# Decode block on one core: output weights of group six behind the last values, second MLP weights in 8, 3, 2, 1 chunks, group two's last query rows by eight DMA engines

## The chip, the cores and the metric

The kernel runs on one core of a Trainium2 chip. The metric is the device time of one execution in microseconds (us), lower is better; the time before is the median of three runs. Loads go through 16 DMA engines of the core; the compute engines are PE (matrix), DVE (vector), ACT (scalar) and POOL. SP does no arithmetic here: it issues the large loads and the final store.

## The reference

One decode step of a transformer block in float32, for 4 tokens (batch B = 4, one query each) and a model width D of 448: grouped attention with 16 query heads over 8 key/value groups of width 256, on the last 1024 entries of the cache, then an MLP of width F = 1792. Each part has a layer norm ahead of it and a residual sum behind it.

```python
def _A_ref(x, k_cache, v_cache, wq, wo):
    W = min(4096, max(256, Sk // 4))          # 1024
    q = (x @ wq) -> heads
    k = k_cache[:, :, Sk - W:, :];  v = v_cache[:, :, Sk - W:, :]
    p = softmax(q @ k^T * Dh ** -0.5)
    return (p @ v) -> rows @ wo
def _B_ref(x, w1, b1, w2, b2):
    return gelu(_layernorm(x) @ w1 + b1) @ w2 + b2
h = x + _A_ref(_layernorm(x), k_cache, v_cache, wq, wo)
out = h + _B_ref(_layernorm(h), w1, b1, w2, b2)
```

Nearly all of the bytes are the keys and values: 8 groups, each 4 MB of keys and 4 MB of values, read once.

## The kernel before

**Loads.** `load` fills a tile of 128 partitions from a packed array in HBM, on SP's queue, in one DMA or in several pieces (L52). There are two rings of two tiles each: kind "k" and kind "v". A load into a tile waits until the work on the tile's earlier contents is done, and each DMA on the queue also waits for the semaphore of the one eight places before it. For group g, `load_k` brings the keys and, in the same rows, the query weights of the next groups (1792 columns); `load_v` brings the values and, in the same rows, the group's output weights `wo` (1792 columns behind the 8192 of the values). The rows of these arrays in HBM are 9984 floats long (39936 bytes).

The query weights of one group are a 448 x 512 matrix. Its first 384 rows lie as 3 x 512 columns on 128 partitions; the last 64 rows are folded onto 128 partitions and 256 columns. Group one is the exception: its last 64 rows come as 64 partitions of 512 columns, by two small DMAs (L73) whose source is shaped (8, 4, 512) with a gap behind each four, so that the outermost dimension is 8. The four small loads of the residual rows and biases (`rows`, L132) go by ACT's queue at the start.

**The loop over the groups.** `scores` (L182) multiplies queries and keys, `transpose_p` turns the softmax, `project_q` (L159) makes the queries of the group two ahead, `values` (L219) multiplies with the values in four pairs of chunks, `transposed_output` (L236 to L244) scales and transposes the result, and `add_output` (L248) adds its product with the output weights into the accumulator `acc`. The last two groups, six and seven, are written out behind the loop.

**The order behind the loop.** The order on PE is the order of the program text; the loads are issued in text order on SP's queue: keys of seven, values of six with their `wo`, values of seven in three pieces, `wo` of seven, the first MLP weights `w1` in two pieces, the second `w2` in three pieces of 8, 4 and 2 chunks (D columns each). PE runs: values of six; the first pair of seven's values; transposition and output of six (L248); a copy of `acc` to `accs` on ACT (L321); two more pairs of seven's values; `add_quadrants` (L256), which folds `accs` into the four-quadrant layout of `last`; the last pair; the transposition of seven; the output of seven added to `last` (L335). Then come the layer norm (L358 to L374), the first MLP product `pu` (L388), the gelu (L402), transposes, and the second product. Its chunks 0 to 7 go into `pa` (L421), which ACT copies to `pas` (L425); chunks 8 to 13 go directly into `py` (L431), and after chunk 9 `add_quadrants` folds `pas` into `py` (L256). The residual is added at L437 and the result stored at L438. `keep_warm` (L308) puts matmuls without a use into waits so that PE's clock stays up.

Of the kernel before, what the change touches and what calls it, by code (L numbers as in the profile page):

```python
# [8 lines left out]
F32 = mybir.dt.float32  # L9
# [6 lines left out]
B, D = 4, 448  # L16
HQ, HKV, SK, DH = 16, 8, 4096, 256
REP = HQ // HKV
W = min(4096, max(256, SK // 4))
F = 1792  # L20
P = 128
H = P // 2
ND = 4
NKC = W // P
NFC = F // P
FQ = F // 4
Q = 32
CACHE = NKC * B * DH
WEIGHTS = 4 * D
# [1 line left out]
SCALE = DH ** -0.5  # L31

@with_exitstack
def block_kernel(ctx: ExitStack, tc, rows, wq0, k0, wq1, kq, vo, w1, w2, out):
    nc = tc.nc
    const = ctx.enter_context(tc.tile_pool(name="const", bufs=1))
    ring = ctx.enter_context(tc.tile_pool(name="ring", bufs=2))
# [10 lines left out]
    def load(kind, src, pieces, name):  # L48
        t = ring.tile([P, CACHE + WEIGHTS], F32, tag=kind, name=name)
        at = 0  # L50
        for n in pieces:
            nc.sync.dma_start(t[:, at : at + n], src[:, at : at + n])  # L52
            at += n
        return t


    def wq_parts(t, last=None):
        parts = [(a, yT[:, a, :], slice(0, 512), t[:, a * 512 : (a + 1) * 512]) for a in range(3)]
        if last is not None:
            return parts + [(3, yT[:H, 3, :], slice(0, 512), last)]  # L60
        for i in range(2):
            parts.append((3, yT[:, 3 + i, :], slice(i * 2 * P, (i + 1) * 2 * P), t[:, 3 * 512 :]))
        return parts


    def load_k(g):
        half = CACHE // 2
        if g == 0:
            t = load("k", k0, (CACHE + 3 * 512,), "k0")


            for i in range(2):
                nc.sync.dma_start(  # L73
                    wq1_last[i * Q : (i + 1) * Q, :], wq1[i].rearrange("e (p c) -> e p c", c=512)[:, :4, :]
                )
            last = wq1_last
        else:
            pieces = (CACHE + WEIGHTS,) if g + 1 < HKV else (CACHE,)
            t = load("k", kq[g - 1], pieces, f"k{g}")
            last = None  # L80
        kt = [t[:, i * half : (i + 1) * half].rearrange("p (c b k) -> p c b k", c=2, b=B) for i in range(2)]
        return kt, wq_parts(t[:, CACHE:], last) if g + 1 < HKV else None


    def load_v(g):
        pieces = (CACHE + WEIGHTS,)
        if g == HKV - 1:
            pieces = (CACHE // 4, CACHE // 2, CACHE // 4, WEIGHTS)
        t = load("v", vo[g], pieces, f"v{g}")
        v = t[:, :CACHE].rearrange("p (c b d) -> p c b d", c=NKC, b=B)  # L90
        return [v[:, c : c + 2] for c in range(0, NKC, 2)], t[:, CACHE:].rearrange("p (j e) -> p j e", j=4)


    ident = const.tile([P, P], F32, name="ident")
# [11 lines left out]

    yT = const.tile([P, ND + 1, Q], F32, name="yT")
    nc.vector.memset(yT, 0.0)
    wq1_last = const.tile([H, 512], F32, name="wq1_last")
    zT = const.tile([P, ND, Q], F32, name="zT")  # L110
    nc.vector.memset(zT, 0.0)

# [62 lines left out]
    def scores(g, kt):  # L175
        mx = work.tile([P, 2], F32, tag="mx", name=f"mx{g}")
        halves = []
        for h in range(2):
            s = ps_s.tile([P, 512], F32, tag="s", name=f"s{g}_{h}")
            for c in range(2):  # L180
                for b in range(B):
                    nc.tensor.matmul(  # L182
                        s[b * Q : (b + 1) * Q, :], qT[g % 2][:, c, b, :], kt[h][:, c, b, :],
                        start=(c == 0), stop=(c == 1),
                    )
            nc.vector.reduce_max(mx[:, h : h + 1], s, axis=AX.X)  # L186
            halves.append(s)
        nm = work.tile([P, 1], F32, tag="nm", name=f"nm{g}")
        nc.vector.tensor_max(nm, mx[:, 0:1], mx[:, 1:2])
        nc.vector.tensor_scalar_mul(nm, nm, -SCALE)  # L190
        p = work.tile([P, 2 * 512], F32, tag="p", name=f"p{g}")
        sums = work.tile([P, 2], F32, tag="sums", name=f"sums{g}")
        for h in range(2):
            nc.scalar.activation(  # L194
                p[:, h * 512 : (h + 1) * 512], halves[h], AF.Exp, bias=nm, scale=SCALE,
                accum_out=sums[:, h : h + 1],
            )
        rec = work.tile([P, 1], F32, tag="rec", name=f"rec{g}")
        nc.vector.tensor_add(rec, sums[:, 0:1], sums[:, 1:2])
        nc.vector.reciprocal(rec, rec)  # L200
        return p, rec
# [14 lines left out]
    def values(g, vt, po, pairs=range(NKC // 2)):  # L216
        for c in pairs:
            for b in range(B):
                nc.tensor.matmul(  # L219
                    po[b * Q : (b + 1) * Q], pT[g % 2][:, c, b, :], vt[c][:, :, b, :],  # L220
                    start=(c == 0), stop=(c == NKC // 2 - 1),
                )
# [5 lines left out]
    def columns(t, j):  # L228
        if j < 3:
            return t[:, j * P : (j + 1) * P].rearrange("p (i c) -> p i c", i=2)  # L230
        return t[:, None, 3 * P :].to_broadcast([t.shape[0], 2, H])


    def transposed_output(g, po, rec):
        o = work.tile([P, 2, DH], F32, tag="o", name=f"o{g}")
        nc.vector.tensor_scalar_mul(o, po, rec)  # L236
        pt = ps_m.tile([P, 2, 2, P], F32, tag="m", name=f"pot{g}")
        for i in range(2):
            for c in range(2):
                nc.tensor.transpose(pt[:, i, c], o[:, i, c * P : (c + 1) * P], ident)  # L240
        dst = oT[g % 2].rearrange("p (r c) q -> p c r q", r=REP)[:, :, :, :B]
        src = pt.rearrange("p i c (b q) -> p i c q b", b=B)
        nc.vector.tensor_copy(dst, src[:, 0, :, :REP])  # L243
        nc.vector.tensor_add(dst, dst, src[:, 1, :, REP : 2 * REP])  # L244

    def add_output(g, wt):
        for i in range(4):
            nc.tensor.matmul(  # L248
                acc[i * Q : (i + 1) * Q, :], oT[g % 2][:, i, :], wt[:, i, :],
                start=(g == 0), stop=(g == HKV - 2),  # L250
            )


    def add_quadrants(dst, t, start):
        for j in range(4):
            nc.tensor.matmul(dst[j * Q : (j + 1) * Q], sel, columns(t, j), start=start, stop=False)  # L256

    def po_tile(g, pool=ps_o, tag="o"):
        return pool.tile([P, 2, DH], F32, tag=tag, name=f"po{g}")


    t = load("v", wq0, (WEIGHTS + ND * B,), "wq0")
    wqt = wq_parts(t[:, :WEIGHTS])
    xT = t[:, WEIGHTS : WEIGHTS + ND * B].rearrange("p (a b) -> p a b", a=ND)
    d = work.tile([P, ND, B], F32, tag="d", name="d_x")
# [11 lines left out]
    p, rec = scores(0, kt)  # L277
    project_q(1, wqt)
    transpose_p(0, p)
    for g in range(HKV - 2):  # L280
        kt, wqt = load_k(g + 1)
        vt, wot = load_v(g)
        p, rec_next = scores(g + 1, kt)
# [8 lines left out]

    g = HKV - 2
    kt, _ = load_k(g + 1)
    vt, wot = load_v(g)
    vt_last, wo_last = load_v(g + 1)
    t = load("k", w1, (2 * F, F + F // 2), "w1")
    w1t = [t[:, a * F : min((a + 1) * F, 3 * F + F // 2)] for a in range(ND)]
    t = load("k", w2, (8 * D, 4 * D, 2 * D), "w2")
    w2t = [t[:, c * D : (c + 1) * D] for c in range(NFC)]  # L300
    p, rec_last = scores(g + 1, kt)

# [3 lines left out]
    def keep_warm(n, warm):  # L306
        for _ in range(n):
            nc.tensor.matmul(warm[:Q], idle[:, :Q], idle, start=True, stop=True)  # L308
# [6 lines left out]
    po_last = po_tile(g + 1, ps_t, "t")  # L315
    warm = ps_t.tile([P, 512], F32, tag="t", name="warm")
    values(g + 1, vt_last, po_last, range(0, 1))
    transposed_output(g, po, rec)
    add_output(g, wot)
    accs = once.tile([P, D], F32, tag="u", name="accs")  # L320
    nc.scalar.copy(accs, acc)  # L321

    keep_warm(2, warm)
    values(g + 1, vt_last, po_last, range(1, 3))
    last = ps_s.tile([P, 512], F32, tag="s", name="last")[:, :P]
    ph = last.rearrange("p (i c) -> p i c", i=2)
    add_quadrants(ph, accs, True)
    values(g + 1, vt_last, po_last, range(3, 4))

    keep_warm(2, warm)  # L330
    transposed_output(g + 1, po_last, rec_last)
    keep_warm(1, warm)
    for i in range(4):
        for j in range(4):
# [27 lines left out]
    d = once.tile([P, P], F32, tag="dh", name="dh")  # L362
# [21 lines left out]
    for a in range(ND):  # L384
        m = Q if a == 0 else B
        for j in range(4):
            rows, w = w1_part(a, j)
# [29 lines left out]
    first = 8  # L417
    pa = ps_w.tile([P, D], F32, tag="acc", name="pa")
    for c in range(first):
        j, m = c % 4, Q if c < 4 else B  # L420
# [6 lines left out]
    for c in range(first, NFC):  # L427
        for j in range(4):
            m, n = (Q, 2) if c == first else (B, 2 if j < 3 else 1)
            w = columns(w2t[c], j) if n == 2 else w2t[c][:, None, 3 * P :]  # L430
            nc.tensor.matmul(  # L431
                py[j * Q : j * Q + m, :n, :], gT[:, c, :m], w, start=(c == first), stop=(c == NFC - 1),
            )
        if c == first + 1:
            add_quadrants(py, pas, False)
    res = once.tile([P, P], F32, tag="res", name="res")
    nc.vector.tensor_add(res, py.rearrange("p i c -> p (i c)"), hb)  # L437
# [67 lines left out]
```

## Time and profile before

| | us |
|---|---|
| median of 3 runs | 214.57 |
| the runs, lowest to highest | 214.44 to 214.58 |
| the profiled execution, first to last instruction | 212.9 |
| PE busy in it | 137.9 |
| DVE busy | 39.2 |
| ACT busy | 21.0 |
| bytes read from HBM | 88.26 MB, 415 GB/s over the span |

The profile is of one execution. Its span leaves out what lies around the first and last instruction, 1.7 us. A line of its timeline gives the start and length of a group of instructions in us, the engine, the line of the kernel, the operation with output and inputs, and in brackets how long the engine had been idle and what ended that. PEld is PE's loading of stationary operands, which runs beside its matmuls; each float32 matmul of the program appears as two in the trace. In a row of stretches stand the stretch, the busy time and count of each engine, the granted PE clock, the mean busy share of the DMA engines and GB/s. A packet is counted in the stretch in which it starts, so the share can pass 1. In the list of DMA queues, q1 holds SP's loads, q8 and q14 the fetches of instructions; the columns are packets, MB and share of the sixteen engines' time.

### The profile page before, as it was taken

How to read it: one execution, taken by the hardware profiler on the slowest of the kernel's cores; microseconds unless marked ns; L12 is line 12 of the kernel's file. 1: busy time of each engine (PE TensorE's matmuls, PEld its weight loads, DVE VectorE, ACT ScalarE, POOL GpSimd, SP SyncE). 2: the span in 40 equal slices, each digit the busy share in tenths (PEclk: the TensorE clock that was granted, in tenths of full speed). 3: DMA queues.
4: the chain of work that ended last, by engine and by line, in shares of the span. 5: the costliest groups of instructions: out<-in, count | busy, mean ns of one | idle time of the engine just before them, and what ended most of it. 6: DMA issues, size and time to landing. Idle time of an engine off the chain costs nothing.

```text
span 212.9 us, 2306 instructions
## 1 busy us (share of the span) xinstructions
PE 137.9 (65%) x971; PEld 49.1 (23%) x971; DVE 39.2 (18%) x167; ACT 21.0 (10%) x52; POOL 5.6 (3%) x17
## 2 busy tenths in 40 slices
PE   0456868093886739583986348382948476798994
PEld 0322233021231212211231113120222123234432
DVE  1420324001130202210130104110230231022320
ACT  0210213000030000300030003000030001000311
POOL 6100000000000000000000000000000000000110
PEclk9999999669597966969599859979797999699999
DMA  7999998999989999999999999999989999999991
GB/s 291 426 399 469 398 465 378 459 465 390 458 378 465 465 390 458 398 446 465 390 458 405 443 465 386 465 413 428 461 375 468 440 428 390 417 418 433 424 390 60
DMA packets 3865, 88.46 MB, mean 415 GB/s; under 512 B 448, under 2 KB 576, under 8 KB 1168
## 3 DMA queue, kind: packets, MB, share of 16 engines
q1 hardware_dynamic: 3824, 88.29, 96.9%
q8 instruction: 7, 0.11, 0.2%
q10 hardware_dynamic: 32, 0.05, 0.1%
q14 instruction: 2, 0.02, 0.0%
HBM read 88.26 MB, written 0.07 MB: 415 GB/s over the span
## 4 chain that ended last, share of the span: by engine, by line
DMA 85%; PE 11%; DVE 2%; issue 0%; SPq 0%
DMA v<-vo 65%; DMA w<-w 12%; DMA k<-k 8%; PE po L219 8%; PE acc L248 1%; DVE o L236 1%; PE pot L240 1%; PE py L431 1%; DVE oT L243 0%; DVE oT L244 0%; SPq L52 0%; DVE res L437 0%; PE py L256 0%
## 5 line engine op out<-in xcount | busy, mean ns | idle before, releaser
L182 PE MATMUL s<-k,qT 128*32 128x512 f32 x256 | 42.3, 822 | 24.7 <-DMA k<-kq 22.6
L219 PE MATMUL po<-v,pT 128*32 128x512 f32 x256 | 40.0, 772 | 19.6 <-DMA v<-vo 19.6
L186 DVE TENSOR_REDUCE mx<-s 128x1 f32<-128x512 f32 x16 | 11.1, 691 | 67.4 <-PE s L182 67.4
L182 PEld LDWEIGHTS s<-k,qT 128*32 128x32 f32 x256 | 10.0, 146 | 54.7 <-issue 29.4
L219 PEld LDWEIGHTS po<-v,pT 128*32 128x32 f32 x256 | 10.7, 135 | 42.3 <-issue 31.4
L161 ACT COPY qs<-pq 128x512 f32<-128x512 f32 x8 | 4.7, 586 | 135.8 <-PE pq L159 135.8
L236 DVE TENSOR_SCALAR o<-po,rec 128x512 f32<-128x512 f32 x8 | 6.0, 750 | 60.2 <-PE po L219 60.2
L194 ACT ACTIVATE p<-s,nm 128x512 f32<-128x512 f32 x16 | 10.9, 690 | 18.4 <-DVE nm L190 18.4
L207 PE MATMUL ppt<-ident,p 128*128 128x128 f32 x64 | 10.5, 286 | 2.0 <-ACT p L194 1.7
L165 PE MATMUL pqt<-ident,qs 128*128 128x128 f32 x32 | 5.7, 304 | 6.2 <-ACT qs L161 6.2
L240 PE MATMUL pot<-ident,o 128*128 128x128 f32 x32 | 5.2, 286 | 5.7 <-DVE o L236 5.7
L248 PE MATMUL acc<-v,oT 128*32 128x448 f32 x56 | 6.7, 551 | 3.3 <-DVE oT L244 3.3
L207 PEld LDWEIGHTS ppt<-ident,p 128*128 128x128 f32 x64 | 6.7, 140 | 6.0 <-ACT p L194 6.0
L159 PE MATMUL pq<-k,yT 128*32 128x512 f32 (+1 forms) x66 | 7.3, 515 | 0.0
L308 PE MATMUL warm<-idle 128*32 128x512 bf16 x25 | 7.3, 382 | 0.0
L240 PEld LDWEIGHTS pot<-ident,o 128*128 128x128 f32 x32 | 3.3, 140 | 13.0 <-DVE o L236 13.0
L165 PEld LDWEIGHTS pqt<-ident,qs 128*128 128x128 f32 x32 | 3.6, 150 | 10.9 <-ACT qs L161 9.1
L153 POOL TENSOR_TENSOR r<-ve_r,mhalf 128x1 f32<-128x1 f32 x2 | 1.1, 544 | 191.9 <-DVE ve_r L152 191.9
L211 DVE COPY pT<-ppt 128x16 f32<-128x16 f32 x32 | 4.7, 170 | 4.7 <-PE ppt L207 4.7
L159 PEld LDWEIGHTS pq<-k,yT 128*32 128x32 f32 x66 | 3.1, 110 | 6.1 <-issue 4.8
L138 PE MATMUL pm_x<-wq,mean 128*128 128x12 f32 x2 | 0.6, 363 | 5.8 <-DMA wq<-wq 5.8
L167 DVE TENSOR_REDUCE sm<-pqt 128x16 f32<-128x64 f32 x8 | 1.8, 225 | 13.0 <-PE pqt L165 13.0
(101 smaller groups left out, 60.9 us busy)
## 6 DMA issues: line engine op xcount, KB each, us to landing
v<-vo SPq DMA_DIRECT2D x7, 4992.0 KB, 31.8
k<-kq SPq DMA_DIRECT2D x6, 4992.0 KB, 32.0
k<-k SPq DMA_DIRECT2D x1, 4864.0 KB, 16.3
k<-kq SPq DMA_DIRECT2D x1, 4096.0 KB
w<-w SPq DMA_DIRECT2D x2, 1792.0 KB
v<-vo SPq DMA_DIRECT2D x2, 1024.0 KB, 22.2
v<-vo SPq DMA_DIRECT2D x1, 2048.0 KB
w<-w SPq DMA_DIRECT2D x1, 1344.0 KB
```

The lines of the kernel that those rows point to most:

```text
L159: nc.tensor.matmul(pq[j * Q : (j + 1) * Q, cols], y, w, start=True, stop=True)
L161: nc.scalar.copy(qs, pq)
L165: nc.tensor.transpose(pt[:, i, :], qs[:, i * P : (i + 1) * P], ident)
L182: nc.tensor.matmul(s[b * Q : (b + 1) * Q, :], qT[g % 2][:, c, b, :], kt[h][:, c, b, :], start=(c == 0), stop=(c == 1),)
L186: nc.vector.reduce_max(mx[:, h : h + 1], s, axis=AX.X)
L194: nc.scalar.activation(p[:, h * 512 : (h + 1) * 512], halves[h], AF.Exp, bias=nm, scale=SCALE, accum_out=sums[:, h : h + 1],)
L207: nc.tensor.transpose(pt[:, c, :], p[:, (4 * h + c) * P : (4 * h + c + 1) * P], ident)
L219: nc.tensor.matmul(po[b * Q : (b + 1) * Q], pT[g % 2][:, c, b, :], vt[c][:, :, b, :], start=(c == 0), stop=(c == NKC // 2 - 1),)
L236: nc.vector.tensor_scalar_mul(o, po, rec)
L240: nc.tensor.transpose(pt[:, i, c], o[:, i, c * P : (c + 1) * P], ident)
L248: nc.tensor.matmul(acc[i * Q : (i + 1) * Q, :], oT[g % 2][:, i, :], wt[:, i, :], start=(g == 0), stop=(g == HKV - 2),)
L308: nc.tensor.matmul(warm[:Q], idle[:, :Q], idle, start=True, stop=True)
```

## The change

Three parts, with the host packing that goes with each.

- The values of groups six and seven lie in an array `v` of their own, with rows of 8192 floats (32768 bytes). The output weights of six and of seven are packed ahead of `w1` in an array `ow`, and are loaded in this order behind seven's last values: `wo` of six, `wo` of seven, `w1` in two pieces. On PE all of seven's values come before the output of six, and the fold of `accs` comes behind seven's transposition.
- `w2` is loaded in pieces of 8, 3, 2 and 1 chunks, and `pas` is folded into `py` after chunk 10.
- The last 64 rows of group two's query weights come, as group one's did, in two small DMAs of the (8, 4, 512) shape, behind the keys of group one; the rows of those keys lose 256 columns.

```diff
+    def load_last(n):
+        t = wq_last[:, n, :]
+        for i in range(2):
+            nc.sync.dma_start(
+                t[i * Q : (i + 1) * Q, :], wql[n, i].rearrange("e (p c) -> e p c", c=512)[:, :4, :]
+            )
+        return t
...
     def load_k(g):
...
-            for i in range(2):
-                nc.sync.dma_start(
-                    wq1_last[i * Q : (i + 1) * Q, :], wq1[i].rearrange("e (p c) -> e p c", c=512)[:, :4, :]
-                )
-            last = wq1_last
+            last = load_last(0)
+        elif g == 1:
+            t = load("k", kq[0], (CACHE + 3 * 512,), "k1")
+            last = load_last(1)
...
     def load_v(g):
-        pieces = (CACHE + WEIGHTS,)
-        if g == HKV - 1:
-            pieces = (CACHE // 4, CACHE // 2, CACHE // 4, WEIGHTS)
-        t = load("v", vo[g], pieces, f"v{g}")
...
+        if g < HKV - 2:
+            t = load("v", vo[g], (CACHE + WEIGHTS,), f"v{g}")
+        else:
+            pieces = (CACHE,) if g == HKV - 2 else (CACHE // 4, CACHE // 2, CACHE // 4)
+            t = load("v", v[g - HKV + 2], pieces, f"v{g}")
...
-    vt, wot = load_v(g)
-    vt_last, wo_last = load_v(g + 1)
-    t = load("k", w1, (2 * F, F + F // 2), "w1")
+    vt, _ = load_v(g)
+    vt_last, _ = load_v(g + 1)
+    t = load("k", ow, (WEIGHTS, WEIGHTS, 2 * F, F + F // 2), "ow")
+    wot, wo_last = (wo_parts(t[:, i * WEIGHTS : (i + 1) * WEIGHTS]) for i in range(2))
+    t = t[:, 2 * WEIGHTS :]
     w1t = [t[:, a * F : min((a + 1) * F, 3 * F + F // 2)] for a in range(ND)]
-    t = load("k", w2, (8 * D, 4 * D, 2 * D), "w2")
+    t = load("k", w2, (8 * D, 3 * D, 2 * D, D), "w2")
...
     transposed_output(g, po, rec)
+    keep_warm(2, warm)
+    values(g + 1, vt_last, po_last, range(1, 4))
+
+    keep_warm(2, warm)
     add_output(g, wot)
     accs = once.tile([P, D], F32, tag="u", name="accs")
     nc.scalar.copy(accs, acc)
-
-    keep_warm(2, warm)
-    values(g + 1, vt_last, po_last, range(1, 3))
+    transposed_output(g + 1, po_last, rec_last)
     last = ps_s.tile([P, 512], F32, tag="s", name="last")[:, :P]
     ph = last.rearrange("p (i c) -> p i c", i=2)
     add_quadrants(ph, accs, True)
-    values(g + 1, vt_last, po_last, range(3, 4))
-
-    keep_warm(2, warm)
-    transposed_output(g + 1, po_last, rec_last)
     keep_warm(1, warm)
...
-        if c == first + 1:
+        if c == first + 2:
             add_quadrants(py, pas, False)
```

More of the change, by code (lines that the diff above doesn't have):

```diff
@@ L33, in block_kernel @@
 @with_exitstack
-def block_kernel(ctx: ExitStack, tc, rows, wq0, k0, wq1, kq, vo, w1, w2, out):
+def block_kernel(ctx: ExitStack, tc, rows, wq0, k0, wql, kq, vo, v, ow, w2, out):
     nc = tc.nc
@@ L82, in load_k, with wo_parts @@
         return kt, wq_parts(t[:, CACHE:], last) if g + 1 < HKV else None
+    def wo_parts(t):
+        return t.rearrange("p (j e) -> p j e", j=4)
     def load_v(g):
-        pieces = (CACHE + WEIGHTS,)
-        if g == HKV - 1:
-            pieces = (CACHE // 4, CACHE // 2, CACHE // 4, WEIGHTS)
-        t = load("v", vo[g], pieces, f"v{g}")
-        v = t[:, :CACHE].rearrange("p (c b d) -> p c b d", c=NKC, b=B)
-        return [v[:, c : c + 2] for c in range(0, NKC, 2)], t[:, CACHE:].rearrange("p (j e) -> p j e", j=4)
+        if g < HKV - 2:
[3 more added lines that the diff above has]
+            t = load("v", v[g - HKV + 2], pieces, f"v{g}")
+        vt = t[:, :CACHE].rearrange("p (c b d) -> p c b d", c=NKC, b=B)
+        return [vt[:, c : c + 2] for c in range(0, NKC, 2)], wo_parts(t[:, CACHE:])
     ident = const.tile([P, P], F32, name="ident")
@@ L108, in block_kernel @@
     nc.vector.memset(yT, 0.0)
-    wq1_last = const.tile([H, 512], F32, name="wq1_last")
+    wq_last = const.tile([H, 2, 512], F32, name="wq_last")
     zT = const.tile([P, ND, Q], F32, name="zT")
@@ L470 @@
     k0 = np.concatenate([k[0], wq[1][:, : 3 * 512]], axis=1)
-    wq1 = np.asarray(A_wq).reshape(D, HKV, 512)[3 * P :, 1].reshape(2, 8, 4 * 512)
-    wq1 = np.concatenate([wq1, np.zeros((2, 8, 512), np.float32)], axis=2)
-    vo = np.concatenate([v, wo], axis=2)
-    w1 = packed(np.asarray(B_w1))
+    wql = np.asarray(A_wq).reshape(D, HKV, 512)[3 * P :, 1:3].transpose(1, 0, 2).reshape(2, 2, 8, 4 * 512)
+    wql = np.concatenate([wql, np.zeros((2, 2, 8, 512), np.float32)], axis=3)
+    vo = np.concatenate([v[: HKV - 2], wo[: HKV - 2]], axis=2)
+    v = v[HKV - 2 :]
+    ow = np.concatenate([wo[HKV - 2], wo[HKV - 1], packed(np.asarray(B_w1))], axis=1)
     w2 = np.asarray(B_w2).reshape(4, FQ, D)
@@ L489 @@
     arrays = {
-        "rows": rows, "wq0": np.concatenate([wq[0], xT], axis=1), "k0": k0, "wq1": wq1, "kq": kq, "vo": vo, "w1": w1, "w2": w2,
+        "rows": rows, "wq0": np.concatenate([wq[0], xT], axis=1), "k0": k0, "wql": wql, "kq": kq, "vo": vo, "v": v, "ow": ow, "w2": w2,
     }
```

## The prediction, made before the changed kernel ran

> **What bounds the kernel now.** I read the page first, then the chain of waits from its end, then the DMA share in stretches, then the timeline of the last stage.
>
> ```profile
> span 212.9 us, 2306 instructions
> PE 137.9 (65%) x971; PEld 49.1 (23%) x971; DVE 39.2 (18%) x167; ACT 21.0 (10%) x52; POOL 5.6 (3%) x17
> DMA  7999998999989999999999999999989999999991
> q1 hardware_dynamic: 3824, 88.29, 96.9%
> q8 instruction: 7, 0.11, 0.2%
> q14 instruction: 2, 0.02, 0.0%
> DMA 85%; PE 11%; DVE 2%; issue 0%; SPq 0%
> ```
>
> The DMA engines are busy in every slice but the last, and 85% of the chain is DMA. So the time is the loads' bytes over their rate, plus what follows the last landing. PE at 65% has room. The chain's last pieces:
>
> ```profile
> 145.34 36.79 DMA v<-vo
> 182.14 26.22 DMA w<-w
> 208.41 0.64 PE py L431 x13
> 209.05 0.17 PE py L256 x6
> 209.22 0.97 PE py L431 x19
> 210.21 0.29 DVE res L437
> ```
>
> The second MLP weights are the last load, and only 2 us of arithmetic stand behind it. How the engines run out of work (columns at the end: DMA share, GB/s):
>
> ```profile
> 132.00:144.00 12.00, 7.70 (x48) 2.69 (x46) 2.04 (x11) 1.04 (x4) 0.00 (x0) 0.86 1.03 443
> 206.50:207.00 0.50, 0.50 (x8) 0.13 (x4) 0.00 (x0) 0.03 (x1) 0.00 (x0) 1.00 0.92 380
> 207.00:207.50 0.50, 0.50 (x12) 0.13 (x4) 0.00 (x0) 0.00 (x0) 0.00 (x0) 1.00 0.75 308
> 207.50:208.00 0.50, 0.50 (x8) 0.00 (x0) 0.00 (x0) 0.00 (x0) 0.00 (x0) 1.00 0.61 244
> 208.00:208.50 0.50, 0.13 (x7) 0.09 (x8) 0.00 (x0) 0.35 (x1) 0.00 (x0) 1.00 0.60 244
> 208.50:209.00 0.50, 0.50 (x24) 0.50 (x28) 0.00 (x0) 0.18 (x1) 0.00 (x0) 1.00 0.17 65
> ```
>
> The sixteen engines do not finish together: from 207 on about 12, then 10, and past 208.5 fewer than 3 still move data. The first are done near 206.8, the last near 208.8, a spread of about 2 us. The slowest engine sets the landing. And the last stage of PE:
>
> ```profile
> 206.33 1.71 PE L421 MATMUL pa<-w,gT 128*32 128x448 f32 x16
> 208.15 0.53 ACT L425 COPY pas<-pa 128x448 f32<-128x448 f32 x1 [1.62 <-PE pa L421]
> 208.78 0.48 PE L256 MATMUL py<-pas,sel 128*32 128x128 f32 x8
> 209.20 0.94 PE L431 MATMUL py<-w,gT 128*4 128x128 f32 x25
> 209.50 0.34 PEld L431 LDWEIGHTS py<-w,gT 128*4 128x4 f32 x16
> ```
>
> The last 16 weight loads (chunks 12 and 13, the last load of w2) begin at 209.50; the data engines stop near 208.9, so I read this start as the last landing. From there to the residual add at 210.21 pass 0.71 us.
>
> **The change part by part. First, w2 in 8, 3, 2, 1 chunks.** Only chunk 13 is then behind the last landing: 8 PE instructions in place of 16. In the row of 25 the starts run from 209.20 to the last start, 0.94 less one duration of 0.27 (the shape's median, 0.27 us for a 128-column matmul): 0.67 us over 24 steps, 28 ns each. Eight fewer: -0.22 us. This needs chunks 11 and 12 and the folding of pas done before. L421 ends at 208.04; chunks 8 to 10 take 24 x 0.028 = 0.67, to 208.71; pas is copied by 208.68; the 8 matmuls of L256 and 16 of chunks 11 and 12 take 0.67 more, to 209.4, just under 209.50. So the gain holds, with 0.1 us of cover; were it gone, the -0.22 would be 0. That is the bound on the other side: 0 to -0.22, taken at -0.22.
>
> The price is a row per partition and DMA more. In rows of 3584 bytes the engines that still run move 244 GB/s at a share of 0.60, 407 for a full share; in rows of 39936 bytes 443 at 1.03, or 430. Per engine that is 141 ns against 133 for 3584 bytes: some 8 ns of fixed cost a row. An engine has 8 rows of each DMA, so one more DMA is at most 0.06 us. It happens twice on all engines (the extra w2 piece, wo of group six split from its v rows); group two's q rows cost about as much again. 0 to +0.2 us, taken at +0.1, since part of the 8 ns is the semaphore write and not the row.
>
> **Second, the output weights of group six.** The 896 KB (0.92 MB) move from inside v6's rows to behind v7's last piece: same bytes, same queue, and the last landing does not move. What lies before them lands earlier by 0.92 MB / 430 GB/s = 2.1 us.
>
> ```profile
> 169.84 0.42 SPq L52 DMA_DIRECT2D v<-vo  x1
> v<-vo SPq DMA_DIRECT2D x1, 1024.0 KB, 22.2
> 170.31 0.43 SPq L52 DMA_DIRECT2D v<-vo  x1
> v<-vo SPq DMA_DIRECT2D x1, 896.0 KB, 24.0
> 182.26 6.20 PE L219 MATMUL po<-v,pT 128*32 128x512 f32 x40 [2.62 <-DMA v<-vo]
> 189.59 0.96 PE L248 MATMUL acc<-v,oT 128*32 128x448 f32 x8 [0.47 <-DVE oT L244]
> 190.62 0.53 ACT L321 COPY accs<-acc 128x448 f32<-128x448 f32 x1 [13.94 <-PE acc L248]
> 195.78 1.08 PE L335 MATMUL last<-v,oT 128*32 128x128 f32 x32 [0.15 <-DVE oT L244]
> 199.54 0.96 PE L388 MATMUL pu<-w,zT 128*32 128x448 f32 x8
> 201.92 1.80 PE L388 MATMUL pu<-w,zT 128*4 128x448 f32 x16
> ```
>
> v7's last piece lands at 169.84 + 22.2 = 192.0, wo7 at 170.31 + 24.0 = 194.3. After the change: v6 at 180.0, v7 complete at 189.9, wo6 at 192.0, wo7 still 194.3. PE's new order waits for v7 and then for wo6: the last pair of value chunks, 8 instructions at 6.20 / 40, ends by 191.2; L248 starts at 192.0 and takes 0.96; behind it in PE's order stand group seven's transposes, the folding of accs (after the 0.53 us copy on ACT) and L335, which needs wo7 at 194.3 anyway. L335 so starts near 194.6, 1.2 us before its 195.78. The MLP cannot use that: its second piece of w1 is 1792 + 1344 KB behind wo7, 3.21 MB / 430 GB/s, 201.8, and the 16 matmuls that need it start at 201.92 already. At most 0.1 us reaches L421, and none the last landing. Net 0; if the cover were gone, the 1.2 us is what PE could lose before it is worse off.
>
> **Third, group two's last 64 query rows by eight engines.** 128 KB that sixteen engines carried are carried by eight: 8 KB less on each of eight, 8 KB more on each of the others. At 430 / 16 = 26.9 GB/s an engine, that is 0.30 us down or up. One project_q matmul goes, under a DMA-bound stage. Two DMAs more on SP's queue stand ahead of v0:
>
> ```profile
> 17.46 0.33 SPq L52 DMA_DIRECT2D v<-vo  x1
> 24.29 0.33 SPq L52 DMA_DIRECT2D k<-kq  x1
> ```
>
> Each DMA takes the semaphore of the one eight places before it, so v0 now waits for group one's small loads rather than for k0, a matter of half a microsecond, while k1's 4.9 MB are under way to about 29 us; k2's issue at 24.29 waits for PE as before. No gap in the data: 0.
>
> Which eight end last decides the sign. Before, the eight already carry 2 x 64 KB alone (16 KB each, 0.6 us) and four of them the 44 KB of rows (0.4 us); all else on the sixteen is even, but for the instruction fetches:
>
> ```profile
> q8 instruction: 1, 0.02, 4.2%
> q14 instruction: 1, 0.01, 1.8%
> ```
>
> These two rows are of the stretch from 202.0 to 203.6: a fetch of 16 KB held one engine for 4.2% of 16 x 1.6 us = 1.1 us, the other for 0.5. Nine of them in the span, spread over sixteen engines, explain a spread of 2 us. A fetched engine of the loaded eight is later than a fetched one of the rest, so the last landing is more likely on a loaded engine: +0.30. The other bound is -0.30.
>
> The Trainium skill (DMA: Bandwidth & Descriptors, section "Why a DMA increments its semaphore by 16 and not by 1") says that an HWDGE transfer of k engines uses the lowest-numbered k. By that, both groups' small loads fall on the same eight, which is the +0.30 case; by a rotating choice they would level out. No run here shows engine numbers.
>
> Sum on the profiled execution: -0.22 + 0.1 + 0 + 0.30 = +0.18 us on a span of 212.9; what lies around the span (214.57 - 212.9 = 1.7) is untouched. **Forecast 214.75 us.**
>
> **The rivals.** (1) The unloaded engines are last. Then -0.22 + 0.1 - 0.30 = -0.42, 214.15. For it: nine fetches can fall on the rest alone, and they then outweigh 1.0 us of load. Against: it needs nearly all to do so.
>
> (2) The values of groups six and seven now come from an array of their own, whose rows are 32768 bytes apart, not 39936. If sixteen streams at that pitch hinder one another in HBM, the load slows in one place, v6 and v7: 8.39 MB, 19.5 us at 430 GB/s. The slowest stretch of the stream shows how far a rate can fall:
>
> ```profile
> 180.00:182.00 2.00, 0.00 (x0) 0.00 (x0) 0.00 (x0) 0.00 (x0) 0.00 (x0) 1.00 0.88 367
> ```
>
> At 367 it would be 22.9 us, +3.4. I price a fall of 3%, less than half the way: +0.6, 215.35; it decides over the forecast's sign from 1.3% on (0.25 us). Against: rows of one array here lie end to end.
> [...]
>
> (3) PE's order turns against it: waiting for v7, wo6 and wo7 in turn, PE idles between 186 and 194 and its clock is halved, as it was after the 2.62 us wait ahead of L219 (the column before DMA share is the granted clock):
>
> ```profile
> 182.00:184.00 2.00, 1.74 (x12) 0.68 (x16) 0.00 (x0) 0.00 (x0) 0.00 (x0) 0.61 1.13 475
> ```
>
> From 189.9 to L335's end PE has some 4.6 us of work (1.3 of values, 0.96, 0.7 of transposes, 0.48, 1.08). Half speed throughout adds 4.6; the waits hide the values' 1.3, L335's 1.2 us of lead takes the next part, and the 0.5 us between 209.4 and 209.9, where PE would wait for chunk 13, the last. 1.6 us are left at worst; I price half: +0.8, 215.55. It decides from a delay of 1.7 us on. Against: each of the three waits is under 2 us.
>
> (4) The smaller pieces do not do what they say: chunks 11 and 12 still run when 13 lands. Then the -0.22 is gone: 214.97, inside the forecast's own range.
>
> **How the numbers follow.** Forecast 0.50, with 214.5 to 215.0 as its own range; rival 1 0.26; rival 2 0.13; rival 3 0.08; the rest, with fetches elsewhere, 0.03. What a measurement of this kernel tells from no change is about 0.2%, 0.43 us: 214.14 to 215.0. Faster takes 0.17 of rival 1 and the rest's 0.03: 0.20. Slower takes 0.06 of the forecast and all of rivals 2 and 3: 0.27. Same: 0.53. The range runs from rival 1 to rival 2: 214.1 to 215.4; rival 3 lies outside it.
>
> **What would show it.** The last load group of L431 should be 8 weight loads, with 0.49 us from it to the residual add (0.71 before); 0.71 again means rival 4. Its start gives the last landing: 209.9 in the forecast, 209.3 in rival 1. The DMA share past 208.5 shows whether the tail grew longer or shorter. L335 near 194.6 confirms the order on PE; later than 195.8 is rival 3. v7's landing near 189.9, from its own issue, speaks against rival 2; beyond 190.5 for it. The forecast is wrong if the landing moves by more than 0.4 us either way.

## The result and the profile after

The changed kernel takes 215.55 us, the median of 12 runs (214.84 to 217.18), against 214.55 for the kernel before on the same chips (12 runs, 214.28 to 214.76). The ratio is 1.005, with a 95% interval of 1.0035 to 1.0065: slower by 0.5%, beyond the forecast of 214.75 and just outside the range. The runs of the kernel before lie within 0.5 us; those of the changed one are spread over 2.3 us. That spread is the second finding beside the median.

The profiled execution of the changed kernel took 214.97 us, one of its shorter ones. Its page, in the lines that answer to those of before:

```profile
span 213.2 us, 2308 instructions
PE 136.1 (64%) x969; PEld 47.4 (22%) x969; DVE 39.2 (18%) x167; ACT 21.0 (10%) x52; POOL 5.6 (3%) x17
DMA  7999999999999999999999999999999999999991
q1 hardware_dynamic: 4192, 88.29, 96.9%
q8 instruction: 7, 0.11, 0.2%
DMA 78%; PE 16%; DVE 2%; SPq 2%; issue 1%; ACT 0%; DVEq 0%
```

The bytes are the same (88.29 MB), in 368 packets more. DMA's share of the chain fell from 85% to 78% and PE's rose from 11% to 16%. A part of this lies early in the chain; at its end, work on PE now follows from the landing of `w1`, near 202.2, where before the last load stood until 208.4. The stretches in which the engines run out of work (last columns: granted PE clock, DMA share, GB/s):

```profile
207.00:207.50 0.50, 0.50 (x12) 0.25 (x8) 0.00 (x0) 0.00 (x0) 0.00 (x0) 1.00 0.79 315
207.50:208.00 0.50, 0.50 (x12) 0.01 (x3) 0.00 (x0) 0.00 (x0) 0.00 (x0) 1.00 0.71 280
208.00:208.50 0.50, 0.50 (x16) 0.32 (x16) 0.00 (x0) 0.05 (x1) 0.00 (x0) 1.00 0.51 197
208.50:209.00 0.50, 0.50 (x20) 0.24 (x12) 0.00 (x0) 0.48 (x1) 0.00 (x0) 1.00 0.24 90
209.00:209.50 0.50, 0.50 (x22) 0.40 (x21) 0.00 (x0) 0.00 (x0) 0.00 (x0) 1.00 0.03 11
```

Past 208.5 the share is 0.24 where it was 0.17, and data still move after 209, where none did. The tail of the load has grown longer. The last stage on PE, from the timeline of the same execution:

```profile
192.63 0.96 PE L261 MATMUL acc<-ow,oT 128*32 128x448 f32 x8 [0.81 <-DMA ow<-ow]
194.79 1.08 PE L348 MATMUL last<-ow,oT 128*32 128x128 f32 x32
202.28 1.80 PE L401 MATMUL pu<-ow,zT 128*4 128x448 f32 x16 [0.75 <-DMA ow<-ow]
206.63 1.71 PE L434 MATMUL pa<-w,gT 128*32 128x448 f32 x16
209.76 0.11 PEld L444 LDWEIGHTS py<-w,gT 128*4 128x4 f32 x8 [0.16 <-DMA w<-w]
210.23 0.29 DVE L450 TENSOR_TENSOR res<-py,hb 128x128 f32<-128x128 f32 x1 [3.71 <-PE py L444]
```

Eight weight loads stand behind the last landing, 0.47 us before the residual add. L348, the output of group seven, starts at 194.79, a microsecond earlier than its 195.78 before. But the second half of the first MLP product waits 0.75 us for w1, to 202.28; before, it started at 201.92 with nothing to wait for.

The residual add comes 0.02 us later than before (210.23 against 210.21), and yet the span is longer by 0.3 us. The rest stands behind the store of the result. The program ends with waits of SP for the semaphores of the DMAs, one after another in a fixed order. These are SP's rows for the store, before and after (us in all, times, longest; the line is that of the program's end):

```profile
SPq L499 <- DMA out<-res: 0.9, 1, 0.9
SPq L513 <- DMA out<-res: 1.2, 1, 1.2
```

The traces hold five such waits. Before, four of them are over by the time the store lands and one is left; in the changed kernel the store's semaphore stands in the first, and the other four follow it, some 0.06 us each. The reason is a count: the DMAs take eight semaphores in turn, and four DMAs more move the store to another one. From the store's issue to the end of the span pass 2.39 us before and 2.64 in the changed kernel (2.64 in each of its three profiles), so 0.25 us of the change come from there.

### The profile page after: what moved, and what is told of

Its sections match the earlier page's. It is cut to its first block, busy times and chain, and to the rows that moved or that the text cites. A ratio compares the mean times of both kernels' runs of the same rounds, so it can differ in the third digit from the quotient of the medians.

```text
span 213.2 us, 2308 instructions
## 1 busy us (share of the span) xinstructions
PE 136.1 (64%) x969; PEld 47.4 (22%) x969; DVE 39.2 (18%) x167; ACT 21.0 (10%) x52; POOL 5.6 (3%) x17
## 3 DMA queue, kind: packets, MB, share of 16 engines
q1 hardware_dynamic: 4192, 88.29, 96.9%
## 4 chain that ended last, share of the span: by engine, by line
DMA 78%; PE 16%; DVE 2%; SPq 2%; issue 1%; ACT 0%; DVEq 0%
DMA v<-vo 56%; DMA ow<-ow 14%; DMA k<-k 8%; PE po L232 7%; PE s L195 2%; SPq L52 2%; PE acc L261 1%; DVE o L249 1%; PE pot L253 1%; PE pu L401 1%; PE pa L434 1%; PE py L444 1%; PE pq L172 0%; PE put L420 0%; DVE oT L256 0%
## 5 line engine op out<-in xcount | busy, mean ns | idle before, releaser
L195 PE MATMUL s<-k,qT 128*32 128x512 f32 x256 | 43.4, 841 | 28.4 <-DMA k<-kq 25.8
L232 PE MATMUL po<-v,pT 128*32 128x512 f32 x256 | 35.0, 693 | 17.4 <-DMA v<-vo 16.5
L195 PEld LDWEIGHTS s<-k,qT 128*32 128x32 f32 x256 | 10.5, 148 | 59.4 <-issue 31.2
L232 PEld LDWEIGHTS po<-v,pT 128*32 128x32 f32 x256 | 8.7, 125 | 38.6 <-issue 24.4
L261 PE MATMUL acc<-v,oT 128*32 128x448 f32 x48 | 5.8, 551 | 2.8 <-DVE oT L257 2.8
L401 PE MATMUL pu<-ow,zT 128*4 128x448 f32 (+2 forms) x32 | 3.7, 541 | 1.2 <-DMA ow<-ow 1.2
```

What stands on the lines that cost most here:

```text
L195: nc.tensor.matmul(s[b * Q : (b + 1) * Q, :], qT[g % 2][:, c, b, :], kt[h][:, c, b, :], start=(c == 0), stop=(c == 1),)
L232: nc.tensor.matmul(po[b * Q : (b + 1) * Q], pT[g % 2][:, c, b, :], vt[c][:, :, b, :], start=(c == 0), stop=(c == NKC // 2 - 1),)
L261: nc.tensor.matmul(acc[i * Q : (i + 1) * Q, :], oT[g % 2][:, i, :], wt[:, i, :], start=(g == 0), stop=(g == HKV - 2),)
L401: nc.tensor.matmul(pu[j * Q : j * Q + m, :], zT[rows, a, :m], w, start=(a == 0), stop=(a == ND - 1),)
```

## The experiments

Two theories and a rival. **L**: the eight DMA engines with the small loads become the last ones, and each such load lengthens the end. **C**: the new order on PE costs it its clock in some executions. **P**: the 32768-byte pitch of the array v slows its load. The parts are numbered as in the section on the change: the first is the output weights of group six, the second `w2`, the third the query rows. First the parts alone, all against the kernel before on the same chip (214.53, 32 runs).

### The change without its third part

```diff
-        elif g == 1:
-            t = load("k", kq[0], (CACHE + 3 * 512,), "k1")
-            last = load_last(1)
```

> The change without its third part (group two's last 64 query rows by sixteen engines again, inside the rows of k1). Theory L, the eight engines that carry the small loads end last and the third part lengthens them: the last landing goes back by about 0.3 us, the median is 214.3 to 214.5 and the runs lie within 0.6 us of one another as before. Theory C, the new order on PE costs its clock in some executions: the median stays near 215.5 with runs up to 217. Theory P, the 32768-byte pitch of v slows its load: as C in the median, but v7 lands later than 190 us in the slow executions.

Measured: 214.65 (11 runs), ratio 1.0016, interval 0.9998 to 1.0033. The median came back by almost all, near what L expected (214.3 to 214.5); but the runs reach from 214.37 to 216.56, as C has it, and not within the 0.6 us of L. Neither alone is enough.

### The third part alone

The same hunk, with `load_last` and its array, put into the kernel before.

> The kernel before with the third part alone. Theory L: slower by 0.3 to 0.9 us, 214.9 to 215.5, runs spread over more than 1 us, and the DMA engines' spread of ends is 2.5 to 3 us where it was 2. Theories C and P: 214.4 to 214.7, with the spread of before.

Measured: 215.01 (10 runs), ratio 1.0023, interval 1.0014 to 1.0033. Slower by 0.48 us, as L expected, but within 214.96 to 215.16, where L expected a spread of more than 1 us: the third part costs time and makes no spread. The timeline of its profile shows `pa`, the first product with w2, late, and its stretches show the longer tail:

```profile
206.65 1.71 PE L429 MATMUL pa<-w,gT 128*32 128x448 f32 x16 [0.20 <-DMA w<-w]
```

```profile
208.50:209.00 0.50, 0.39 (x16) 0.35 (x16) 0.00 (x0) 0.50 (x1) 0.00 (x0) 1.00 0.22 86
209.00:209.50 0.50, 0.50 (x30) 0.44 (x21) 0.00 (x0) 0.01 (x1) 0.00 (x0) 1.00 0.06 22
```

Before, `pa` began at 206.33, and nothing moved after 209. From the store's issue to the end pass 2.55 us, so 0.16 of the 0.48 are the waits behind the store and 0.32 are left for the load.

### The second part alone

```diff
-    t = load("k", w2, (8 * D, 4 * D, 2 * D), "w2")
+    t = load("k", w2, (8 * D, 3 * D, 2 * D, D), "w2")
...
-        if c == first + 1:
+        if c == first + 2:
```

> The kernel before with w2 in 8, 3, 2, 1 chunks alone, pas folded after chunk 10. All theories: 8 weight loads behind the last landing, 0.49 us from their start to the residual add where it was 0.71; 214.3 to 214.5.

Measured: 214.41 (11 runs, 214.36 to 214.66), ratio 0.9997, interval 0.9988 to 1.0006: 0.12 us lower in the median, not told from none. One DMA more lengthens the stretch behind the store to 2.48 us, 0.09 more than before; without this the gain would be 0.21. Its timeline has the predicted form, 0.47 us from the last eight weight loads to the residual add:

```profile
209.42 0.11 PEld L431 LDWEIGHTS py<-w,gT 128*4 128x4 f32 x8 [0.22 <-DMA w<-w]
209.89 0.29 DVE L437 TENSOR_TENSOR res<-py,hb 128x128 f32<-128x128 f32 x1 [3.97 <-PE py L431]
```

### The first part alone

The changed kernel without the third part's hunk and with w2 again in 8, 4 and 2 chunks, pas folded after chunk 9.

> The kernel before with the first part alone: wo of group six behind seven's values, v in an array of its own, the new order on PE. Theory L: 214.5 to 214.7, since PE's lead ends at w1's landing. Theories C and P: 215 to 216 with runs up to 217.

Measured: 214.73 (11 runs), ratio 1.0019, interval 1.001 to 1.0028, in two groups: 214.51 to 214.73 and 215.10 to 215.29. L expected the one (214.5 to 214.7); C and P expected 215 to 216. So the first part makes the spread. The profiled execution took 215.23 and shows half the clock for one stretch of 3.4 us (columns: PE, PEld, DVE, ACT, POOL busy, granted clock, DMA share, GB/s):

```profile
196.41:199.83 3.42, 2.74 (x21) 1.34 (x24) 0.59 (x4) 2.09 (x5) 0.00 (x0) 1.00 1.01 425
199.83:203.24 3.41, 3.41 (x18) 0.64 (x18) 0.67 (x4) 0.00 (x0) 1.09 (x2) 0.50 1.02 432
```

### Two more profiles of the changed kernel

The kernel is the changed one as it stands.

> The changed kernel again, one more profile. Theory C: where this execution takes 215.4 us or more, the granted clock is 0.5 in a stretch of 3.4 us that begins between 197 and 206, and the chain of waits runs through PE from the first MLP product to the end; where it takes less, the clock stays at 1.0 from 186 on.

> As the look before, a second profile of the changed kernel: at 215.4 us or more the clock is 0.5 in a stretch between 197 and 206; below that it stays at 1.0.

The first took 214.92 us, the second 215.53, on one chip. The shorter one, in stretches (columns as above), and from its timeline:

```profile
197.10:200.52 3.42, 2.88 (x20) 1.27 (x24) 0.62 (x3) 1.97 (x5) 0.02 (x1) 1.00 1.01 424
200.52:203.93 3.41, 2.68 (x27) 0.58 (x20) 0.59 (x3) 0.00 (x0) 1.07 (x2) 1.00 1.02 429
```

```profile
198.96 0.96 PE L401 MATMUL pu<-ow,zT 128*32 128x448 f32 x8 [0.47 <-DMA ow<-ow]
200.16 0.94 PE L401 MATMUL pu<-ow,zT 128*4 128x448 f32 x8
202.14 1.80 PE L401 MATMUL pu<-ow,zT 128*4 128x448 f32 x16 [0.73 <-DMA ow<-ow]
```

The longer one:

```profile
196.73:200.14 3.41, 2.73 (x17) 1.26 (x16) 0.67 (x4) 2.09 (x5) 0.00 (x0) 1.00 1.01 426
200.14:203.56 3.42, 3.42 (x19) 0.72 (x19) 0.59 (x3) 0.00 (x0) 1.09 (x2) 0.50 1.03 426
```

```profile
198.96 0.96 PE L401 MATMUL pu<-ow,zT 128*32 128x448 f32 x8 [0.49 <-DMA ow<-ow]
200.16 1.67 PE L401 MATMUL pu<-ow,zT 128*4 128x448 f32 x8
202.28 2.40 PE L401 MATMUL pu<-ow,zT 128*4 128x448 f32 x16
207.23 1.71 PE L434 MATMUL pa<-w,gT 128*32 128x448 f32 x16
```

Up to 200.16 the two do the same work at the same times. In the longer one the clock is 0.50 from 200.14 to 203.56: the second chunk of the product takes 1.67 instead of 0.94, the last two 2.40 instead of 1.80, and `pa` starts at 207.23. The chain that ended last (start, length, what) now is PE from the product to the end, not a load:

```profile
202.35 2.38 PE pu L401 x16
204.76 0.06 issue
204.82 0.50 DVE u L414
205.34 0.42 ACT u L415
205.81 0.84 PE put L420 x6
...
207.23 1.75 PE pa L434 x16
209.06 0.54 ACT pas L438
...
210.79 0.29 DVE res L450
```

The residual add begins at 210.79, against 210.21 in the kernel before. In each trace the clock changes only at steps of 3.41 us, and these steps lie 0.4 us apart in the two executions (196.73 and 197.10, the second counted on from the changes earlier in its trace). In the one the stretch holds 17 matmuls and 2.73 us of PE work, in the other 20 and 2.88: the second chunk's eight begin at 200.16, just behind the end of the one stretch and inside the other.

### More keep_warm in PE's waits

```diff
-    keep_warm(1, warm)
+    keep_warm(2, warm)
     h = once.tile([P, P], F32, tag="h", name="h")
...
             nc.vector.tensor_mul(s, s, r1)
+            keep_warm(3, warm)
```

Eight matmuls more, in places where PE waits, in the change without its third part and in the whole change (the diff shows two of the five places). The kernel before took 214.56 on this chip (27 runs), as in the next two experiments.

> Parts one and two, with 8 more keep_warm matmuls in PE's waits of the layer norm and of the first MLP product (2, 2, 2 and 3 where 1 stood, and 3 more ahead of its third chunk). Theory C (PE's clock is halved in the stretch that starts near 199.8 because PE does too little in the 3.4 us before it): the granted clock stays at 1.0 from 186 us to the end, the slow executions go, all runs lie within 214.2 to 214.7 and the median is 214.35. Rival, the slow executions come from the load (pitch of v, fetches): median and spread stay as without them, 214.65 and up to 215.3 or more.

> The whole change with the same 8 more keep_warm matmuls. Theories L and C together: only the load's cost is left, 214.8 to 215.1, spread under 0.4 us. If the spread of 2.3 us stays, its cause is not the clock.

Measured: 214.46 for parts one and two (11 runs, ten of them in 214.33 to 214.62, one at 215.40; ratio 1.0, interval 0.9991 to 1.0008) and 215.04 for the whole change (11 runs, 214.83 to 215.25; ratio 1.0018, interval 1.0009 to 1.0027). The added work lowers the whole change by 0.51 us and its spread from 2.3 to 0.4, to the range of the changed kernel's five shorter runs (214.84 to 215.25). The one run at 215.40 is no halved clock: its span is 212.7 us like the others', and the time lies outside the span. In the profiles of both the clock stays at 1.0 through the MLP. That of the first shows the stretch full of work, and full clock behind it:

```profile
194.91:198.33 3.42, 3.39 (x31) 1.63 (x22) 1.42 (x7) 0.98 (x5) 0.00 (x0) 1.00 1.01 429
198.33:201.74 3.41, 3.41 (x26) 1.10 (x25) 0.59 (x3) 1.11 (x1) 0.63 (x2) 1.00 1.03 430
```

### The kernel before with less keep_warm

The four single `keep_warm(1, warm)` of the layer norm are taken out.

> The kernel before without the four single keep_warm matmuls of the layer norm. Theory C: the clock is halved in the MLP in part of the executions also in this order; runs of 214.5 and runs of 215 to 217 mixed, median over 214.8. Rival (clock irrelevant): 214.4 to 214.7 throughout.

Measured: 216.79 (4 runs, 216.21 to 217.12), ratio 1.01, interval 1.0086 to 1.0114. It is no mixture: all four are long. The clock is halved in two stretches on end:

```profile
194.92:198.33 3.41, 2.00 (x38) 1.44 (x37) 1.43 (x8) 0.40 (x2) 0.00 (x0) 1.00 0.99 419
198.33:201.74 3.41, 3.14 (x16) 1.28 (x20) 0.33 (x2) 1.69 (x3) 0.05 (x1) 0.50 1.03 434
201.74:205.15 3.41, 3.41 (x22) 0.69 (x18) 0.59 (x3) 0.00 (x0) 1.04 (x2) 0.50 0.98 407
```

So the clock in the MLP can decide the end in the old order as well, and 216 to 217 us, which the changed kernel reaches in 2 of 12 runs, is what two such stretches cost here. That those two runs had two is inferred; neither was profiled.

### Nothing by eight engines alone

```diff
-            t = load("k", k0, (CACHE + 3 * 512,), "k0")
...
+            t = load("k", k0, (CACHE + WEIGHTS,), "k0")
+            last = None
```

> The kernel before with group one's last 64 query rows too in the rows of k0, so by sixteen engines; nothing goes by eight engines alone. Theory L as the prediction put it (the loaded eight end last by a margin): faster by 0.2 to 0.3 us, 214.2 to 214.35. Rival, that the eight were level with the others before and the third part tips them over: 214.5 to 214.9, no gain or a loss.

Measured: 214.72 (11 runs, 214.61 to 214.88), ratio 1.0008, interval 1.0 to 1.0017. Taking 8 KB off each of the eight and giving it to the others makes the kernel no faster. Of the 0.16 us by which it is slower, 0.11 stand behind the store (2.50 us from its issue to the end: two DMAs fewer also move its semaphore), and in the profile the residual add begins at 210.17, where it was 210.21. So in that execution the load ends when it did. In the kernel before, the eight were then not last by a margin, and the two halves were about level; this is inferred from the times, since no run shows which engine ends last.

### The third part twice

```diff
+        elif g == 2:
+            t = load("k", kq[1], (CACHE + 3 * 512,), "k2")
+            last = load_last(2)
```

> The kernel before with the third part done twice: the last 64 query rows of groups two and three by eight engines each. Theory L (the eight engines are the last ones, and each such step lengthens them by 16 KB in rows of 2 KB less the 8 KB they had): the second step adds as much as the first alone, 0.35 to 0.5 us, 215.35 to 215.5 in all, with a spread under 0.4 us. Rival (the first step's cost is the extra DMAs on SP's queue ahead of v0, not the balance): the second step, which stands elsewhere in the queue, adds under 0.15 us, 215.0 to 215.15.

Measured: 215.52 (5 runs, 215.41 to 215.86), ratio 1.0047, interval 1.0033 to 1.006. The kernel before took 214.53 on this chip too (15 runs), so the second step adds 0.51 us to the first one's 0.48; 0.09 of it are waits behind the store (2.64 us against 2.55). The rival named in the expectation, with under 0.15 us, falls. Its stretches show a tail that grows again, 0.16 of the engines past 209 where the third part once had 0.06:

```profile
208.50:209.00 0.50, 0.32 (x4) 0.00 (x0) 0.00 (x0) 0.06 (x1) 0.00 (x0) 1.00 0.30 122
209.00:209.50 0.50, 0.31 (x12) 0.31 (x16) 0.00 (x0) 0.47 (x1) 0.00 (x0) 1.00 0.16 65
```

### The rows of v padded

```diff
-    v = v[HKV - 2 :]
+    v = np.concatenate([v[HKV - 2 :], np.zeros((2, P, WEIGHTS), np.float32)], axis=2)
```

> Parts one and two with the 8 more keep_warm matmuls, and the rows of the array v padded from 32768 to 39936 bytes, the pitch that the values had before; the padding is not loaded. Theory P, the pitch slows the load of v: faster than the same kernel without the padding (214.46) by 0.3 us or more. Theories L and C: no difference, 214.35 to 214.6.

Measured: 214.62 (11 runs), ratio 1.0006, interval 0.9997 to 1.0015, against 214.46 without the padding. No gain from it, so theory P falls. The profiles agree: the last pair of seven's values starts at 189.89 with the padding and at 189.82 without it.

## Why the prediction was wrong

**The sum that the runs give.** Each row is a median less that of the kernel before on the same chip, in us. What lies behind the store is read from the profiles, from the store's issue to the end of the span, less the 2.39 of the kernel before. The last column is what the prediction had.

| | measured | behind the store | rest | predicted |
|---|---|---|---|---|
| second part (`w2`) | -0.12 | +0.09 | -0.21 | -0.22, and a third of the +0.1 for rows |
| third part (query rows) | +0.48 | +0.16 | +0.32 | +0.30, and a third of the +0.1 |
| the third part's second step | +0.51 | +0.09 | +0.42 | |
| parts one and two, more keep_warm | -0.10 | +0.15 | -0.25 | -0.22, and two thirds of the +0.1 |
| whole change, more keep_warm | +0.48 | +0.25 | +0.23 | +0.18 |
| whole change | +1.00 | +0.25 | +0.75 | +0.18 |

So the sum for the load, +0.18, was nearly right (+0.23 with the clock held up). Two terms are missing from it: 0.51 us of clock (215.55 less 215.04) and 0.25 us behind the store. The last landing, 209.76 where 209.9 was foretold, agrees.

**The step that failed** is the net 0 of the output weights of group six, the second step of the prediction's sum (the change's first part). Its times were right: L348 at 194.8 where 194.6 was worked out, and the lead of a microsecond does end at w1's landing. What was overlooked is what PE does with the lead. It spends it waiting inside the MLP, 0.5 us before the first chunk and 0.7 before the third, next to a layer norm in which it has little to do. A 3.4 us stretch can then fall on that quiet part, and the MLP behind it runs at half clock. The prediction took the lead for cover against lateness; it gave the idle time no price of its own. `only_part1` and the pair of profiles show the halved clock where the time is long, `after_warm` shows the cost gone when the waits are filled, and `before_cold` shows it come in the old order when work is taken out.
What the clock adds to a median hangs on how many executions are halved. In the five profiles with the new order and no added keep_warm, the two long ones (215.23 and 215.53) had the halved clock and the three short ones did not. Of the 12 runs of the whole change 7 took 215.5 us or more, and the median stands among them; without the third part 3 of 11 runs were long, and the median stands among the others. Whether the third part makes the halving more frequent, or this is chance, is open.

**A term that was left at nothing** is what stands behind the residual add. The sum ends there and takes the rest as unchanged, but the waits behind the store go with the number of DMAs, which the change raises by four, and they cost 0.25 us. No run changed that number alone; the cost is read from the traces.

**Rival 3** had the mechanism, at the wrong place and with the wrong reason against it. It looked for the half clock among the waits for v7, wo6 and wo7, ahead of L348, where a delay of 1.7 us had to pass before it decided, and it argued that each wait was under 2 us. The clock falls behind L348. There the cover is the 0.73 us wait before the third chunk and about 0.2 us before chunk 13 (0.16 in the first profile), and the longest wait in the quiet stretch of the longer execution is 0.49 us. It had 0.08 and 215.55 us, by chance the time measured.

**The third part** had its sign and, without the waits behind the store, its size right: 0.32 for 0.30 and about a third of the +0.1. The reason given for the sign does not hold for the kernel before: there the eight engines were about level (`sixteen`), and by the same reading it took the next 16 KB to make them last. With two loads of a kind the first may level and the second tip over; the argument from the load alone (1.0 us more on some) left out that the instruction fetches can fall on the others. The prediction had v0 issued half a microsecond later; it was 1.7 us (19.16 against 17.46), but this left no gap: the DMA share from 14 to 30 us is 1.00 where it was 0.98.
The Trainium skill (DMA: Bandwidth & Descriptors, section "Why a DMA increments its semaphore by 16 and not by 1") has such transfers on the lowest-numbered eight each time. The runs agree as far as they go: by changing engines the two steps would not add 0.32 and 0.42 to the load.

**The second part** was right in form (eight loads, 0.47 us for the predicted 0.49) and in size, 0.21, of which the waits behind the store took back 0.09. **Rivals 2 and 4** fall: padding the rows of v gains nothing, and the weight loads of chunk 13 waited 0.16 us for their data when those of 11 and 12 were done. **Rival 1** falls with the sign of the third part.

No version beats both kernels clearly. The second part alone, 214.41, is the lowest median, but its interval against the kernel before holds 1.

## What to carry to other kernels

Where the load bounds the end, making a compute engine early turns its lead into waiting, and waiting next to a quiet stage can cost PE its clock; take profiles of several executions, since one can miss it, and put filler matmuls into the new waits. Count what stands behind the last store as well: here the number of DMAs decided how many of the closing waits came after it. Before loading some DMA engines more than others, test both directions: a step that leaves them level may tip them over when repeated. A spread that grows with a change is a finding in its own right: here it showed the half of the cost that a single profile hid.

## What the runs showed of the hardware

The granted clock was halved for 3.42 us after a 3.41 us stretch with 2.73 us of PE work and no gap over 0.5 us, and kept after one with 2.88 us, 0.4 us later in phase. The busy time of the page is no threshold by itself: its matmul ends are modelled, and the stretch from 200.52 in the shorter execution had 2.68 us and kept the clock, with 27 matmuls, as did one of 2.55 us with 19 from 201.54 in the first profile. More work in the waits kept the clock up and less lost it; which quantity decides is not shown.
The Trainium skill (TensorE: Matmul & The Clock Gate, section "Why this matters for your kernels") warns of idle gaps over about 3 us; here short gaps in a row were enough, and the measurement decides. The Trainium skill (the same page, section "What's actually happening") also has these stretches run freely, whatever the kernel does, and the pair of profiles agrees, with 196.73 against 197.10.
